# Single PSUM banks for the first two feed-forward units, and a new written order, in a BigBird attention and gated FFN kernel

## The chip, the core and the metric

The kernel runs on one core of a Trainium2 chip. The metric is the device time of one launch in microseconds (us). Before the change three runs took 278.1, 278.68 and 278.46 us, so the median is 278.46 us.

## The reference

Attention over 4 batches, 8 heads, 768 positions and 64 features per head, with a mask over blocks of 32 x 32 (a window of one block, the first and last block, and three sampled blocks per row of blocks), and behind it a feed-forward network (FFN) with a sigmoid gate on 3072 tokens of 512 features:

```python
scores = q @ k.T / 8;  scores = where(mask, scores, -1e9)
attn = exp(scores - max) / (sum + 1e-9);  x = (attn @ v) as tokens x 512
out = (sigmoid(x @ w_gate) * (x @ w_val)) @ w_out      # 512 -> 1536 -> 512
```

## The kernel before

**Units.** A unit is one batch and 256 queries; there are 12 of them, numbered 0 to 11 (three per batch). In a unit the 8 heads form 4 pairs, and each pair takes three key steps of 256 keys. A step is four score matmuls on TensorE (`scores`, through `tiled`, L352) into a PSUM tile of two banks, one exp of 128x1024 on ScalarE (L586), and one multiplication by the mask on VectorE (L592). Unit 0 does without that multiplication: its mask is a bias that four further matmuls add to the scores. A pair ends with its product with V (`pv` or `pv_parts`), a fold (L646) and a division (L656, the "norm").

**FFN.** When the four pairs of a unit are transposed into `xT`, jobs `f` compute gate and value columns: 16 matmuls with 512 columns out per bank, then a tanh (ScalarE, L801) and the gate (VectorE, L804), both on 128x512. Jobs `y` multiply by `w_out`; an evacuation (L886 or L888) and a store follow. Units 0 to 3 have FFN groups of their own, the others go in groups of two. Unit 0's FFN and the V products of units 0 and 1 use the whole 128x128 array, everything else of weight uses row tiles of 64 rows, two at a time.

**Masks and inputs.** The mask tiles are built by matmuls and copied to SBUF (`mask_tiles`, through the helper `copy`: L297 on ScalarE, L299 on VectorE). For batch 0, GpSimd's DMA queue brings q, k, v and the weights in the order of `FIRST`; TensorE transposes q and k (L467, L472), and VectorE copies V into `vex` (`vcopy`, L545). For batches 1 to 3 the loads are spread over the batch before them; VectorE lays two heads side by side (`pair_up`, L525, the "pair copy" into `qp` or `kp`) and SyncE's queue transposes that into `qT` or `kT` by DMA (`xbar`, L536). The same queue transposes `x` into `xT` from unit 2 on (L706) and stores the output (L878).

**PSUM.** Four tiles m0 to m3 of two banks each. Every job takes one of them and holds it until its evacuation.

**Order.** Nothing here is scheduled by the program at build time: some 1170 tasks are issued in the order of the string `ORDER`. A token is a task number, perhaps with an engine's letter, a PSUM tile after a colon, and after an @ the task that a load has to wait for. Tokens that begin with j are idle matmuls at the start. Each engine therefore takes its own instructions in the order in which `ORDER` names their tasks, and waits by semaphores for the others. The costs beside the tasks, such as `(PE, F_HALF)`, are left over from the search that wrote the string; they set nothing in the program that is built.

```python
self.last[i] = fn(eng or engines[0][0])
if gate is not None:
    self.hold(self.last[i], self.last[int(gate)])
```

Of the kernel before, what the change touches and what calls it, by code (L numbers as in the profile page):

```python
# [22 lines left out]
NT = S // 128  # L23
# [8 lines left out]
PE, ACT, DVE, DMA, SP = "PADGS"  # L32
# [4 lines left out]
EARLY = 2  # L37
# [3 lines left out]
j3 j3 j3 j3 j3 j3 j3 j3 5A 8D j3 0 11A j3s 9:0 j3s j3s j3s 10D j3s j3s 12:1 1:2 j3s 13A 3:0 2 j3s 34:1 4D 35 15:2  # L41
j3s 32:3 16D 6:0 33 17:1 7D 117:2 18D 97:0 118D 44:1 98A j3s 22:3 78:2 23D 45 36:0 79D 20:3 37 21D
40:2 25:1 30:3 41 26D 76:0 77D 46:1 31 54:2 19 74:0 47 75D 27:3 24 55 50:0 28D 80:1 64:3 51 81D
48:2 65 60:1 49 56:0 61 14 66:3 58:2 67D 105@30 57 29 89:3 59 38:1 90 52:0 86:2 53D 87 39 68:3
93:0 69D 62:1 108:2 94 42:3 109 43D 102:0 63D 111:3 70:1 103 110 126:2 71D 112 104 95:0 84:1 96D
122:3 85A 113 140:0 127 123 91 130:1 128 132:3 141 129 131 72:2 119:0 99:1 73D 133 120 147:2 134
100 135 142 157:0 148 154:3 171:1 124 155 149 158 88 164:3 143:2 156 176:0 92@164 144 121 146@111
101 172 170@44 165 173 161:2 217@54 145 190:1 177 189@46 162 125@40 178 237@54 159 186:3 191 150:2
115:0 151D 192 174:2 187 116 204:1 175 188 231:0 179:3 183:2 232 205 180D 244:3 184 233 206 166
245 82:0 200:2 218 83D 201 246 234:3 193:0 219 194A 152 235 185 153 211:2 136:0 220 137D 212 138  # L50
272:3 195 139 229 223A 202 167:0 255:2 168 236 273 213 221A 239 214:0 230 307:1 274 169 215 275
256 240 216 197:3 308 257 196 181 198 258 248:0 309 182 199 241:2 249 242 310 268:3 262 225:1 250
260 114@268 263 269 251 252:2 226 318:0 261 207:3 319 253 315:1 208 289:2 316 160@315 254 106:0
265:3 243 290 107A 247@265 266 270 276:1 209 291 300:0 293:3 277 301 278 282:1 294 292 283 297 163
303:0 335:2 295 302 222 304 279 227 285:1 336 296 286 238 359:0 305 337 360 210 284 331:3 228
362:1 348 332 361 264 349 363 333 328:0 287 350 329 267 322:3 351A 320 344:1 353A 311:0 323
203@344 345 341:2 387:3 321@359 312 342 317 271@282 426:1 373:0 313 411@300 427 330 397:2 374 398
343 388 346 375 259 408:1 376 389 355:2 400@268 409 390 347@30 419:0 356 334@89 380:3 405:1 428
370:2 381 306@111 364 420 288@44 406 371 386@214 366:3 421 410 365@265 454:2 422 433:1 455 432@380
# [3 lines left out]
442 474:1 484:0 463A 378 465A 339 467:2 452 340 475 524:3 480 485 525 514 354 515:1 327 468 486  # L63
# [4 lines left out]
538 583 438 550:1 567 571 542 439 586 551 638:0 563:2 572 425 539 564 552 595:1 573A 404 577:2 604  # L68
639 574 596 578 609:0 568 597 555 575A 627:2 598 616:3 610 628 617 543@616 635:1 565 712@200 630:2
611 569@300 636 612 592:3 446@563 688:0 631 593 658@60 689 654 706:1 556@231 588:3 707 579 641@550  # L70
640 642:0 632 676@471 619:1 633 589 587@282 620 594 691@214 623:2 690 613 590 670:1 591 643 671
637 605:3 624 644 621 606 645 659:1 618 625 709:0 681:3 710 626 660 607 655:2 682 692:0 656 453
663:3 711 726@99 661 657 608@234 673:2 693 662 674 622@652 664 672 694 548 699:1 695 665 723:2 666
# [3 lines left out]
762 669 782 730:3 745A 734:0 760 757:2 731 735 753 798:3 703 758 799 732 736 764:0 759 750 743A  # L77
600 765 797 826:3 823:1 767 763 824 650 816:0 766 651 827 809:1 756 768 810 719 800 787:3 817 769
733 788 806:1 801:0 807 770D 819:3 789 772A 811 737:1 790:2 839 738 614 802 580 615 791 803 601
# [5 lines left out]
904 856 925 936:0 978:1 913 937 911 857 919:3 979 908 875:0 920 914 876 929:1 921 917A 905 932  # L85
970:3 930 935 971 877 922 946:0 915A 1024:3 931 947 893 1025 928 1027:2 1012:0 939 938 916 1013
948 959:3 1028 966 1040:0 940 960 1041 1026 941 967:2 973:3 944A 942D 968 945 1029 952:0 1001:1
# [6 lines left out]
1078 1074 1094 1008 1082 1095 1083 1084 1100:1 1087A 1096A 1108:3 1088 1098A 1101 1085A 1099 1097  # L94
# [19 lines left out]

class Bank:


    def __init__(self):
        self.slot = None


class Plan:

# [13 lines left out]
    def run(self):  # L137
        done = set()
        for token in self.order:
            if token[0] == "j":  # L140
                self.idle(int(token[1]), token[2:])
                continue
# [1015 lines left out]
```

## Time and profile before

| | before |
|---|---|
| median of three runs | 278.46 us |
| span of the profiled execution | 277.8 us |
| TensorE (PE) busy | 270.0 us, 97%, 5007 matmuls |
| VectorE (DVE) busy | 207.1 us, 75%, 421 instructions |
| ScalarE (ACT) busy | 192.1 us, 69%, 243 instructions |
| GpSimd (POOL) busy | 47.3 us, 17% |
| granted TensorE clock | 1.00 from the start up to 240 us, 0.99 behind |

The profiled execution has a span of 277.8 us; the median lies 0.66 us above it, for what lies around the span and for the difference between executions. Matmuls overlap, so the duration of one is not what it adds: the pace is read from the distance of two starts. In the timeline a row "x6" stands for six instructions in a run, and the brackets at its end name the idle time ahead of it and what ended it.

### The profile page before, as it was taken

How to read it: one execution, taken by the hardware profiler on the slowest of the kernel's cores; microseconds unless marked ns; L12 is line 12 of the kernel's file. 1: busy time of each engine (PE TensorE's matmuls, PEld its weight loads, DVE VectorE, ACT ScalarE, POOL GpSimd, SP SyncE). 2: the span in 40 equal slices, each digit the busy share in tenths (PEclk: the TensorE clock that was granted, in tenths of full speed). 3: DMA queues.
4: the chain of work that ended last, by engine and by line, in shares of the span. 5: the costliest groups of instructions: out<-in, count | busy, mean ns of one | idle time of the engine just before them, and what ended most of it. 6: DMA issues, size and time to landing. Idle time of an engine off the chain costs nothing.

```text
span 277.8 us, 11169 instructions
## 1 busy us (share of the span) xinstructions
PE 270.0 (97%) x5007; PEld 178.7 (64%) x5007; DVE 207.1 (75%) x421; ACT 192.1 (69%) x243; POOL 47.3 (17%) x69
## 2 busy tenths in 40 slices
PE   8879999999999999999999999999999999999995
PEld 3667785896897798655566655655655676555543
DVE  4667788899999989978988886887876899004422
ACT  3988868899989958968868965679688571035300
POOL 7776261030480000028300000000000000000000
PEclk9999999999999999999999999999999999999999
DMA  7999999994599693339986743014130002230004
GB/s 160 175 195 197 200 205 198 140 139 100 84 160 145 117 140 97 103 98 167 142 113 113 73 61 97 2 21 142 24 96 4 4 2 76 70 151 2 0 2 151
DMA packets 56684, 28.93 MB, mean 104 GB/s; under 512 B 33036, under 2 KB 53692, under 8 KB 56636
## 3 DMA queue, kind: packets, MB, share of 16 engines
q0 software_dynamic: 21520, 13.90, 35.7%
q1 hardware_dynamic: 34628, 14.02, 24.8%
q8 instruction: 39, 0.64, 1.0%
q10 hardware_dynamic: 488, 0.30, 0.3%
q14 instruction: 9, 0.07, 0.1%
HBM read 28.47 MB, written 6.29 MB: 125 GB/s over the span
## 4 chain that ended last, share of the span: by engine, by line
PE 87%; DMA 7%; POOL 2%; ACT 1%; DVE 1%; issue 1%; SPq 0%
PE m L352 86%; DMA q<-in_q_dram 3%; DMA v<-in_v_dram 2%; DMA kT<-kp 1%; ACT P L586 1%; POOL k L226 1%; POOL q L226 1%; POOL wg L236 0%; POOL wv L236 0%; DVE ysb L888 0%; DVE P L592 0%; ACT ysb L886 0%; PE m L472 0%; PE m L467 0%; ACT ysb L929 0%
## 5 line engine op out<-in xcount | busy, mean ns | idle before, releaser
L586 ACT ACTIVATE P<-m 128x1024 f16<-128x1024 f32 x144 | 143.1, 1025 | 27.8 <-PE m L352 24.6
L352 PE MATMUL m<-xT,wg 64*128 64x512 f16 (+2 forms) x720 | 136.7, 326 | 0.1
L352 PE MATMUL m<-xT,wv 64*128 64x512 f16 (+2 forms) x720 | 136.7, 326 | 0.0
L592 DVE TENSOR_TENSOR P<-P,mask 128x1024 f16<-128x1024 f16 x132 | 87.0, 684 | 2.7 <-ACT P L586 2.6
L352 PEld LDWEIGHTS <-wg 64*128 64x128 f16 (+1 forms) x720 | 66.6, 94 | 21.2 <-issue 0.8
L352 PEld LDWEIGHTS <-wv 64*128 64x128 f16 (+1 forms) x720 | 66.4, 94 | 18.2 <-issue 0.5
L804 DVE SCALAR_TENSOR_TENSOR ht<-th,m 128x512 f16<-128x512 f32 x72 | 49.0, 685 | 37.0 <-ACT th L801 36.1
L352 PE MATMUL m<-wo,ht 64*128 64x512 f16 (+2 forms) x564 | 70.4, 372 | 0.0
L801 ACT ACTIVATE th<-m 128x512 f32<-128x512 f32 x72 | 42.8, 598 | 29.6 <-PE m L352 26.1
L352 PE MATMUL m<-qT,kT 64*128 64x256 f16 x576 | 53.6, 269 | 0.9 <-DMA kT<-kp 0.5
L352 PEld LDWEIGHTS <-P 64*128 64x128 f16 (+1 forms) x2112 | 41.1, 94 | 5.2 <-issue 0.4
L352 PEld LDWEIGHTS <-ht 64*128 64x128 f16 (+1 forms) x564 | 29.4, 94 | 23.4 <-issue 1.3
L352 PE MATMUL m<-vex,P 64*128 64x65 f16 (+1 forms) x2112 | 42.5, 190 | 0.0
L352 PEld LDWEIGHTS <-kT 64*128 64x128 f16 x576 | 26.7, 94 | 17.8 <-issue 1.3
L646 DVE TENSOR_REDUCE acc<-m 128x260 f32<-128x520 f32 x40 | 27.8, 697 | 7.9 <-PE m L352 6.8
L226 POOL DMA_DIRECT2D k<-in_k_dram x15 | 11.1, 744 | 48.3 <-PE m L352 45.0
L886 ACT ACTIVATE ysb<-m 128x512 f32<-128x512 f32 x18 | 10.2, 601 | 11.8 <-PE m L352 11.8
L656 DVE TENSOR_TENSOR x<-acc,rz 128x256 f16<-128x256 f32 x40 | 17.0, 425 | 1.4
L226 POOL DMA_DIRECT2D v<-in_v_dram x16 | 11.6, 736 | 33.5 <-PE m L352 12.9
L226 POOL DMA_DIRECT2D q<-in_q_dram x19 | 13.9, 733 | 3.9 <-DMA wo<-in_moe_w_out_dram 1.8
L352 PE MATMUL m<-bias,e 64*128 64x256 f16 x48 | 5.9, 271 | 2.3 <-DVE mask L299 1.9
L929 ACT ACTIVATE ysb<-m 128x256 f32<-128x256 f32 x1 | 0.4, 383 | 10.1 <-PE m L352 10.1
(47 smaller groups left out, 84.1 us busy)
## 6 DMA issues: line engine op xcount, KB each, us to landing
out_dram<-ysb SPq DMA_DIRECT2D x23, 256.0 KB, 2.4
v<-in_v_dram POOLq DMA_DIRECT2D x16, 192.0 KB, 5.1
k<-in_k_dram POOLq DMA_DIRECT2D x15, 192.0 KB, 6.6
q<-in_q_dram POOLq DMA_DIRECT2D x12, 192.0 KB, 6.4
wg<-in_moe_w_gate_dram POOLq DMA_DIRECT2D x6, 256.0 KB, 8.4
wv<-in_moe_w_val_dram POOLq DMA_DIRECT2D x6, 256.0 KB, 9.0
wo<-in_moe_w_out_dram POOLq DMA_DIRECT2D x3, 512.0 KB, 12.8
xT<-x SPq DMA_TRANSPOSE x40, 2.4
```

The costliest lines, as they stand in the source:

```text
L226: return nc.gpsimd.dma_start(dst[:, h0:h1, t0:t1, :], src[b, h0:h1].rearrange("h (p t) d -> p h t d", t=NT)[:, :, t0:t1, :],)
L352: return nc.tensor.matmul(out, lhsT, rhs, start=start, stop=stop, skip_group_check=True).ins
L586: nc.scalar.activation(self.pt.rearrange("a h i n -> a (h i n)"), both(self.bank).rearrange("a h n -> a (h n)"), AF.Exp, bias=0.0, scale=SCALE
L592: nc.vector.tensor_tensor(self.pt, self.pt, m.unsqueeze(1).broadcast_to([128, 2, 2, UQ]), op=ALU.mult,)
L646: nc.vector.tensor_reduce(self.acc.rearrange("a h s d -> a (h s d)"), self.parts.rearrange("a r n -> a n r"), axis=mybir.AxisListType.X, o ...
L656: nc.vector.tensor_tensor(self.x16.rearrange("a s h d -> a h s d"), self.acc[:, :, :, 0:D], rz.broadcast_to([128, 2, 2, D]), op=ALU.mult,)
L801: nc.scalar.activation(th, both(bank)[:, 0, :], AF.Tanh, bias=0.0, scale=0.5)
L804: nc.vector.scalar_tensor_tensor(self.ht[:, tiles[0] : tiles[-1] + 1, :], in0=th.rearrange("a (f n) -> a f n", n=self.w), scalar=1.0, in1= ...
L886: nc.scalar.activation(ysb, both(bank)[:, s, :], AF.Copy, bias=0.0, scale=0.5)
L929: nc.scalar.activation(ysb, src, AF.Copy, bias=0.0, scale=0.5)
```

## The change

- **PSUM** becomes one tile `m` of eight banks. A slot 0 to 3 is a pair of banks as before; a slot a to h is one bank.
- **FFN of units 0 and 1** (`SMALL` = 2) goes by a new job `f1`: one block of 128 gate and value columns in one bank, 8 matmuls of the whole array with 256 columns each, a tanh of 128x256 and a gate of 128x256. There are 24 such jobs for 12 jobs before. Unit 1 changes from row tiles to the whole array by it. The first four jobs of unit 0 (`EARLY`) are split, six matmuls on the first three pairs and two on the fourth.
- **Single banks** are also taken by the V products of units 0 and 1, by the transposes of TensorE (one 128x128 transpose instead of four 64x64 ones, where the string says so), by some mask tiles and by the last outputs.
- **The pair copy** of a batch now depends on the DMA transpose of the same heads of the batch before (`turned_b`).
- **The costs** of the search are replaced by other numbers, and `ORDER` by another string: idle tokens go from 19 to 12, one large evacuation (`mb24`) goes from VectorE to ScalarE, and GpSimd's loads get other tasks to wait for.

The core of the diff, without the string and the numbers:

```diff
-EARLY = 2
+EARLY, SMALL = 4, 2
...
-    units_ps = [ps.tile([128, 2, 512], f32, name=f"m{i}") for i in range(4)]
+    banks = ps.tile([128, 8, 512], f32, name="m")
+    units_ps = [banks[:, 2 * i : 2 * i + 2, :] for i in range(4)]
...
+    def one(bank):
+        i = "abcdefgh".index(bank.slot)
+        return units_ps[i // 2][:, i % 2, :]
...
+    rings["th1"] = [t[:, c : c + UQ] for t in rings["th"] for c in (0, UQ)]
...
+            if bank.single:
+                if flat:
+                    nc.tensor.transpose(one16(bank)[:, i * 128 : (i + 1) * 128], tile_, ident)
+                    continue
...
+        def f1(self, f):
+            bank = Bank()
+            i = len(used["th1"])
+            th = home("th1", i)
+            def go(cs):
+                def mm(eng):
+                    for c in cs:
+                        for g in range(2):
+                            bank.last = tiled(
+                                one(bank)[:, g * UQ : (g + 1) * UQ],
+                                (wg, wv)[g][:, c, f * 128 : (f + 1) * 128],
+                                self.x[:, c, :],
+                                c == 0 and g == 0,
+                                c == 3 and g == 1,
+                            )
+                return mm
+            def tanh(eng):
+                nc.scalar.activation(th, one(bank)[:, 0:UQ], AF.Tanh, bias=0.0, scale=0.5)
+            def gate(eng):
+                nc.vector.scalar_tensor_tensor(
+                    self.ht[:, f, :], in0=th, scalar=1.0,
+                    in1=one(bank)[:, UQ : 2 * UQ], op0=ALU.add, op1=ALU.mult,
+                )
...
         def f(self, j):
+            if self.g < SMALL:
+                for f in range(self.per * j, self.per * (j + 1)):
+                    self.f1(f)
+                return
...
-            a = pair_up(nm, *((k16, kp) if nm == "k" else (q16, qp)), b, p, [ld] + old)
+            a = pair_up(nm, *((k16, kp) if nm == "k" else (q16, qp)), b, p, [ld] + old + turned_b.get((nm, p), []))
...
+            turned_b[nm, p] = [c]
```

**VectorE, the first V copies (about 11 to 18 us of the profile before).** `vex0<-v16` is a copy of one pair's V behind its load, `mask<-m` a mask tile's evacuation, `x16n` the norm of pair n of unit 0. Before:

```order
L299 CAST mask_75<-m0_129 128x2x256
L545 COPY vex0_84<-v16_83 128x12x64
L299 CAST mask_75<-m0_129 128x2x256
L545 COPY vex0_84<-v16_83 128x12x64
L299 COPY qT0_86<-m3_132 128x2x2x64
L299 CAST mask_75<-m1_130 128x2x256
L655 RECIPROCAL rz_477<-m2_131 128x4
L656 TENSOR_TENSOR x161_149<-m2_131,rz_477 128x2x2x64
```

And after the change, at the same place:

```order
L304 CAST mask_75<-m_129 128x2x256 x2
L581 COPY vex0_84<-v16_83 128x12x64
L304 CAST mask_75<-m_129 128x2x256 x2
L581 COPY vex0_84<-v16_83 128x12x64
L691 RECIPROCAL rz_435<-m_129 128x4
L692 TENSOR_TENSOR x160_145<-m_129,rz_435 128x2x2x64
```

Before, the first copy is that of pair 1 (task 19), whose V is loaded second, and pair 1 is the first to be divided. After, it is that of pair 0 (task 14), and pair 0 (`x160`) goes first. All four first mask casts stand ahead of or just behind the first copy on VectorE, and none stands among the first exps on ScalarE any more, which now has the cast of `mb24` ahead of its first exp.

**SyncE's queue, the last transposes of batch 2 (about 105 to 120 us before).** `qT0` and `kT0` are the transposed q and k of batch 2, `xT` the transposed x of the FFN, `out` a store. Before:

```order
L706 DMA_TRANSPOSE xT1_160<-x165_153 128x2x128
L706 DMA_TRANSPOSE xT1_160<-x163_151 128x2x128
L706 DMA_TRANSPOSE xT1_160<-x164_152 128x2x128
L536 DMA_TRANSPOSE qT0_86<-qp_81 128x6x128
L536 DMA_TRANSPOSE kT0_88<-kp_82 128x6x128
L878 DMA out_0_dram<-ysb2_164 128x512
```

After:

```order
L572 DMA_TRANSPOSE kT0_88<-kp_82 128x6x128
L741 DMA_TRANSPOSE xT0_156<-x162_147 128x2x128
L572 DMA_TRANSPOSE kT0_88<-kp_82 128x6x128
L572 DMA_TRANSPOSE qT0_86<-qp_81 128x6x128 x2
L966 DMA out_0_dram<-ysb2_161 128x512
L741 DMA_TRANSPOSE xT1_157<-x164_149 128x2x128
L741 DMA_TRANSPOSE xT1_157<-x160_145 128x2x128
```

Before, the last q and k of batch 2 stand behind ten rows of `xT1` transposes and stores that follow the other six; after, all eight of batch 2 stand ahead of the `xT1` transposes.

**VectorE, the first gates (about 27 to 35 us before).** `ht0<-th` is a gate, `P<-P,mask` a multiplication by the mask. Before:

```order
L592 TENSOR_TENSOR P2_135<-P2_135,mask_75 128x1024
L592 TENSOR_TENSOR P13_146<-P13_146,mask_75 128x1024
L804 SCALAR_TENSOR_TENSOR ht0_157<-th0_154,m2_131 128x2x256
L655 RECIPROCAL rz_741<-m1_130 128x4
L656 TENSOR_TENSOR x165_153<-m1_130,rz_741 128x2x2x64
L299 COPY qT0_86<-m2_131 128x2x4x64
L804 SCALAR_TENSOR_TENSOR ht0_157<-th1_155,m3_132 128x2x256
```

After:

```order
L628 TENSOR_TENSOR P12_142<-P12_142,mask_75 128x1024
L834 SCALAR_TENSOR_TENSOR ht0_154<-th1_152,m_129 128x256
L834 SCALAR_TENSOR_TENSOR ht0_154<-th0_151,m_129 128x256
L691 RECIPROCAL rz_672<-m_129 128x4
L692 TENSOR_TENSOR x164_149<-m_129,rz_672 128x2x2x64
L628 TENSOR_TENSOR P2_132<-P2_132,mask_75 128x1024
L834 SCALAR_TENSOR_TENSOR ht0_154<-th1_152,m_129 128x256
```

Each gate has become two of half the width. Counted down VectorE's whole list in units of a full gate (two small ones are one), the 18th gate has 45 mask multiplications ahead of it in both kernels, the 24th has 60 before and 64 after, the 30th 75 and 78, the 42nd 99 in both: in between the new order runs attention ahead of the FFN. TensorE's matmuls are 5007 before and 4837 after, the difference being transposes and idle matmuls; its changes between row tiles, whole array and the small transposes' tiles are 39 before and 41 after.

More of the change, by code (lines that the diff above doesn't have):

```diff
@@ L31 @@
 NU = S // UQ
-PE, ACT, DVE, DMA, SP = "PADGS"
+PE, ACT, DVE, DMA, SP, ONE = "PADGSQ"
 VB = 5
@@ L429 @@
         ),
-        [(DVE, 0.42)],
+        [(DVE, 0.335)],
     )
     t_rows = [
-        rows(S, lambda eng, spread: copy(eng, mb24, spread), [(DVE, 0.95), (ACT, 0.82)])
+        rows(S, lambda eng, spread: copy(eng, mb24, spread), [(DVE, 0.87), (ACT, 0.70)])
     ]
@@ L438, in mask_tiles, with half @@
         bank = Bank()
+        w = c1 - c0
+        def half(i):
+            return one(bank)[:, i * w : (i + 1) * w] if bank.single else both(bank)[:, i, 0:w]
         def mm(eng):
@@ L744, in scores @@
         a = plan.add(
-            [(PE, (0.44 if first else 0.22) * len(run))],
+            [(PE, (0.433 if first else 0.217) * len(run))],
             mm,
@@ L753, in scores @@
             e = plan.add(
-                [(ACT, 0.98)], st.exp, [a] + before("P", 3 * pr.i + st.j), free=st.bank
+                [(ACT, 0.903)], st.exp, [a] + before("P", 3 * pr.i + st.j), free=st.bank
             )
@@ L844, in f @@
                     take=bank,
-                    lag=GAP,
-                    ops=16 * self.per,
+                    needs=wneeds,
                 )
                 a = plan.add(
-                    [(PE, F_HALF)], half(False), [a], ops=16 * self.per
+                    [(PE, 0.863 if self.w == 512 else 0.872)], half(False), [a], turn=True
                 )
             used["xT"][self.g].append(a)
-            c = plan.add([(ACT, 0.57)], tanh, [a] + before("th", i), free=bank, part=1)
-            g = plan.add([(DVE, 0.68)], gate, [c], free=bank, part=1)
+            old = before("th", i)
+            if i < len(rings["th"]) and used["th1"]:
+                old = [x for m in (2 * i, 2 * i + 1) for x in used["th1"][max(k for k in used["th1"] if k % 6 == m)]]
+            c = plan.add([(ACT, 0.477)], tanh, [a] + old, free=bank)
+            g = plan.add([(DVE, 0.598)], gate, [c], free=bank)
             used["th"][i] = [g]
@@ L898, in part @@
                     take=bank if first and f0 == 0 else None,
-                    lag=0.0 if f0 < 8 else GAP if first else None,
-                    ops=16,
+                    turn=not first and f0 == 0,
+                    needs=(f"o{f0 // 4}",),
                 )
@@ L940, in store @@
                 [after],
[L941 removed]
+                dma="O",
             )
@@ L970, in y_last @@
                         take=bank if f0 == 0 else None,
-                        lag=0.0 if f0 < 8 else None,
-                        ops=8,
-                        wide=True,
+                        one=True,
+                        mode="W",
                     )
```

308 lines of the change are left out of this document (170 added, 138 removed), and 49 rows, old and new, of the table ORDER.

## The prediction

> **What bounds the kernel now.** I read the page first, then TensorE's waits, then the start of the timeline, then a table of stretches. The page:
>
> ```profile
> span 277.8 us, 11169 instructions
> PE 270.0 (97%) x5007; PEld 178.7 (64%) x5007; DVE 207.1 (75%) x421; ACT 192.1 (69%) x243; POOL 47.3 (17%) x69
> PE   8879999999999999999999999999999999999995
> ```
>
> TensorE is busy for 97% of the span and, from the fourth of the forty slices (21 us) to the last but one, for nine tenths or more of each. So the time is TensorE's own work plus what it waits; the change can win at the start, in a few waits, and nowhere else, because it leaves TensorE's arithmetic as it is. The waits of TensorE (total, times, longest):
>
> ```profile
> PE m L352 <- DVE mask L299: 1.9, 1, 1.9
> PE m L329 <- DVE junk L206: 1.0, 1, 1.0
> PE m L352 <- DMA kT<-kp: 0.5, 1, 0.5
> PE m L352 <- DVE x L656: 0.3, 1, 0.3
> PE m L472 <- DMA q<-in_q_dram: 0.2, 1, 0.2
> ```
>
> One wait of 1.9 us for a mask cast is half of all. The timeline shows how it comes about, beginning with a piece of the chain of waits (the landing of the first pair's V), and what it does to ScalarE:
>
> ```profile
> 6.34 6.93 DMA v<-in_v_dram
> ...
> 6.73 1.94 ACT L586 ACTIVATE P<-m 128x1024 f16<-128x1024 f32 x2 [0.86 <-PE m L352]
> 8.56 0.59 ACT L297 CAST mask<-m 128x512 f16<-128x512 f32 x1
> 9.17 5.69 ACT L586 ACTIVATE P<-m 128x1024 f16<-128x1024 f32 x6
> 14.35 0.36 DVE L545 COPY vex<-v 128x768 f16<-128x768 f16 x1 [1.53 <-DMA v<-in_v_dram]
> 14.63 0.68 DVE L299 CAST mask<-m 128x512 f16<-128x512 f32 x1
> 15.36 0.29 PE L352 MATMUL m<-bias,e 64*128 64x256 f16 x2 [1.91 <-DVE mask L299]
> 16.01 4.82 ACT L586 ACTIVATE P<-m 128x1024 f16<-128x1024 f32 x5 [1.15 <-PE m L352]
> 23.94 0.28 PE L352 MATMUL m<-xT,wg 128*128 128x256 f16 x1
> ```
>
> V of the first pair has landed at 6.34 + 6.93 = 13.27 us, yet VectorE stands until 14.35 for the V of the second, which it copies first; a mask cast is queued behind the copy, TensorE waits for the cast's PSUM tile until 15.36, and ScalarE then waits 1.15 us for scores. The twelve exps of unit 0 are pushed back by that and by the cast at 8.56, and the first FFN matmul starts at 23.94.
>
> **The start.** After the change VectorE copies V of pair 0 first, the casts of ScalarE among the exps are gone, and TensorE takes the V product of pair 0 first. Within a run the exps follow each other by (5.69 - 1.03) / 5 = 0.93 us (one takes 1.03, the group row below). If nothing interrupts them the twelfth ends at 6.73 + 11 x 0.93 + 1.03 = 18.0 us. Before, it is the fourth of the run at 16.01, with (4.82 - 1.03) / 4 = 0.95 us each: 16.01 + 3 x 0.95 + 1.03 = 19.9. The gap of 1.9 is the most that the start can give, and agrees with TensorE's wait of 1.91. Two things are taken off. ScalarE now casts `mb24` (128x768) ahead of its first exp; its 128x512 cast took 0.59, and it was idle 0.86 us ahead of that exp, so I charge 0.15 for the part that may not fit. And TensorE will still wait a little, for the third pair's transposes or for the casts that now stand ahead of the first copy: V lands at 13.27, a copy of 0.36 and a cast of 0.68 can still come one behind the other ahead of TensorE's next job, so that I charge 0.45, between nothing (the V product is queued late enough) and 1.04 (copy and cast both late). That makes -1.9 + 0.15 + 0.45 = **-1.3 us**, from -1.9 to -0.7. The weights hold it up no further: TensorE waits for none of them in the list above, and the first FFN job only comes from 23.9 to about 22.
>
> **The small jobs.** TensorE's work is the same: 8 matmuls of 256 columns on the whole array, for half of 16 on half of the rows with twice the columns. What the split costs lies on the evacuating engines:
>
> ```profile
> L801 ACT ACTIVATE th<-m 128x512 f32<-128x512 f32 x72 | 42.8, 598 | 29.6 <-PE m L352 26.1
> L929 ACT ACTIVATE ysb<-m 128x256 f32<-128x256 f32 x1 | 0.4, 383 | 10.1 <-PE m L352 10.1
> L804 DVE SCALAR_TENSOR_TENSOR ht<-th,m 128x512 f16<-128x512 f32 x72 | 49.0, 685 | 37.0 <-ACT th L801 36.1
> 5.60 0.42 DVE L427 TENSOR_SCALAR bias<-m 128x256 f16<-128x256 f32 x1 [0.21 <-PE m L413]
> 30.00:65.00 35.00, 35.00 (x691) 28.01 (x691) 30.19 (x63) 29.81 (x39) 7.85 (x11) 1.00 1.17 170
> ```
>
> The trace has no gate of 128x256; its nearest rows are the 0.42 of a VectorE operation on 128x256 from PSUM and ScalarE's 0.383. Twenty-four small ones for twelve: VectorE 24 x 0.42 - 12 x 0.685 = +1.9 us, ScalarE 24 x 0.383 - 12 x 0.598 = +2.0 us. These jobs lie in the stretch from 30 to 65 us (columns of the last row: time, length, then busy of PE, PEld, DVE, ACT, POOL, the clock, DMA), where VectorE is idle for 35 - 30.19 = 4.8 us and ScalarE for 5.2. So I cost them at nothing; half a PSUM tile also comes free sooner. If the cover is gone, all of it, 2 us, is late.
>
> [...]
>
> **The V products, transposes and changes of mode.** The V products of units 0 and 1 keep their 24 matmuls. A change of the array's tiles costs TensorE something: in three rows on end,
>
> ```profile
> 25.05 0.27 PE L352 MATMUL m<-xT,wg 128*128 128x256 f16 x1
> 25.16 0.27 PE L352 MATMUL m<-xT,wv 128*128 128x256 f16 x1
> 25.36 0.23 PE L467 MATMUL m<-const,x 64*128 64x64 f16 x4
> ```
>
> starts are 0.11 us apart in one mode and 0.20 across the change: 0.09 us. There are 41 changes for 39, +0.2; from 0 (they fall where TensorE waits anyway) to 0.5, if the whole-array transposes, longer than the small ones, aren't hidden either. I take **+0.2 us**. [...]
>
> **The later waits.** Near 122 us TensorE waits for the last k of batch 2:
>
> ```profile
> 117.37 1.24 SPq L536 DMA_TRANSPOSE qT<-qp x1
> 118.66 1.29 SPq L536 DMA_TRANSPOSE kT<-kp x1
> 121.35 0.90 PE L352 MATMUL m<-vex,P 64*128 64x65 f16 x48
> 122.78 0.39 PE L352 MATMUL m<-qT,kT 64*128 64x256 f16 x4 [0.53 <-DMA kT<-kp]
> 200.00:240.00 40.00, 39.88 (x690) 24.50 (x686) 29.74 (x57) 22.43 (x29) 0.00 (x0) 1.00 0.15 44
> ```
>
> The transpose is issued at 118.66, done by 122.78. After, it stands ahead of the `xT1` transposes and stores that it followed, so I count the wait as gone: -0.53, and -0.1 for the run-out of the V product's pipeline in front of it. In the stretch from 200 to 240 us TensorE is short of 40 - 39.88 = 0.1 us, which may go too. Together **-0.7 us**, from -0.7 to 0 (another transpose late in its stead). The new dependency of the pair copy on the batch before holds up VectorE's queue only if that transpose is still under way; batches are some 60 us apart, so I cost it at nothing. What could be queued behind such a wait are mask multiplications.
>
> **VectorE between 87 and 111 us.** This is what speaks against the change:
>
> ```profile
> L592 DVE TENSOR_TENSOR P<-P,mask 128x1024 f16<-128x1024 f16 x132 | 87.0, 684 | 2.7 <-ACT P L586 2.6
> 33.52 2.49 DVE L592 TENSOR_TENSOR P<-P,mask 128x1024 f16<-128x1024 f16 x4
> 86.90 0.69 DVE L804 SCALAR_TENSOR_TENSOR ht<-th,m 128x512 f16<-128x512 f32 x1
> 111.16 0.69 DVE L804 SCALAR_TENSOR_TENSOR ht<-th,m 128x512 f16<-128x512 f32 x1
> 65.00:87.00 22.00, 22.00 (x498) 17.45 (x496) 20.59 (x40) 20.08 (x25) 8.62 (x12) 1.00 0.83 125
> 87.00:111.00 24.00, 24.00 (x642) 19.74 (x640) 22.36 (x48) 19.68 (x24) 0.00 (x0) 1.00 0.70 117
> ```
>
> The gates at 86.90 and 111.16 are the 18th and the 24th. Between them the new order puts four more mask multiplications on VectorE (60 to 64 ahead of the 24th, 45 ahead of the 18th in both). A run of four takes 2.49, so each adds (2.49 - 0.68) / 3 = 0.60 us: 4 x 0.60 = 2.4 us in a stretch in which VectorE is idle for 24 - 22.36 = 1.6 us. If all of that idle time can be used, 0.8 us are too much and gates come late by it, and TensorE with them; if none, 2.4. Work can also move into the stretch ahead, with 22 - 20.59 = 1.4 idle, which the small jobs' gates leave alone, and PSUM tiles in hand let TensorE run on. I take **+0.9 us**, near the lower end, because VectorE's idle time in this kernel mostly waits for something (the group rows: gates for the tanh 36.1 us) that comes earlier when TensorE is itself held.
>
> **Sum.** Of the profiled execution's 277.8 us: -1.3 + 0.2 - 0.7 + 0.9 = -0.9, so 276.9; the median of the runs shown is 0.66 above the span, 278.46, so 278.46 - 0.9 = 277.56, said as **277.6 us**. With the terms' good ends (-1.9, 0, -0.7, +0.8) it is 276.7, with the bad ends (-0.7, +0.5, 0, +2.4) 280.7. About 0.2%, 0.56 us, is what a measurement of this kernel can tell from no change.
>
> **Rivals.**
> 1. *VectorE becomes the bound between 65 and 115 us.* None of its idle time is usable, the four multiplications cost 2.4 us, and 0.9 of the 1.9 us of the small gates is pushed in front of them: 3.3 us for 0.9. Then the sum is -1.3 + 0.2 - 0.7 + 3.3 = +1.5: 280.0 us. For it: 93% busy in the stretch. Against it: the multiplications are ahead of need, so that a late one need not stop TensorE. It decides from about 2.4 us of waits, where the gains are used up. In the milder half of it, waits of some 2.6 to 2.9 us, 279.2. Chance 0.28.
> 2. *The start's gain is lost again.* TensorE meets another wait ahead of the first FFN matmul, for the second half of q (the waits list has 0.2 us for it even now) or for a bank that a small tanh still holds; the start gives 0.2 rather than 1.3, and the sum is +0.2: 278.6 us. For it: DMA is full in the first 40 us, and an earlier TensorE meets the same landings. Against it: 1.4 us of waits for weights or q would have to appear where 0.2 are. Chance 0.14.
> 3. *One tile instead of four.* If waits were made for the whole tile `m` rather than for its banks, each job would wait for every other's evacuation, and the banks would not be independent: the change would not do what it says, and the time would rise by tens of us, since each exp of 1.03 us would stop TensorE. The order's waits show none of this kind, so only 0.02, outside the range.
>
> The forecast's own case, with 276.7 to 278.4 as its range, has the remaining 0.56; in a part of it, 0.07, the waits at VectorE are 1.5 to 1.9 and the time is within 0.2% of before. The bounds: **276.6 to 280.0 us** reach to the first rival. Faster by over 0.2%: 0.49. Within: 0.07, with 0.10 of the second rival: 0.17. Slower by over 0.2%: 0.28 + 0.02 + 0.04 = 0.34.
>
> **What the profile after would show.** Right: no idle TensorE of over 0.6 us between 12 and 16 us; twelve exps on end from 6.7 to 6.9 us on ScalarE; the first FFN matmul at 22 to 22.7; no wait for `kT<-kp` at 120; waits for VectorE of about 0.9 us between 87 and 120. Wrong: the first FFN matmul at 23.5 or later (second rival); waits for mask multiplications or gates of over 2.4 us in the list (first rival); a `qT` or `kT` wait at another place, which would bring back the 0.7.

## The result, and the profile after

| | before | after |
|---|---|---|
| median of four runs | 278.57 us | 289.34 us |
| runs | 278.1, 278.46, 278.68, 278.98 | 285.49, 286.62, 292.06, 293.16 |
| ratio, 95% interval | | 1.026 (1.0218 to 1.0303) |
| span of the profiled execution | 277.8 us | 284.9 us |

The forecast was 277.6, with 280.0 as its upper end: it is wrong, in sign and in range. Two runs of after (292.06, 293.16) had a granted clock of 0.99 on average and are left out of the ratio, which would be 1.039 with them (289.34 / 278.57); the profiled one, 286.62, is not one of them.

The page of after, with the fortieths of the span for TensorE (PE) and for the DMA engines:

```profile
span 284.9 us, 10851 instructions
PE 272.2 (96%) x4837; PEld 182.9 (64%) x4837; DVE 208.8 (73%) x433; ACT 192.2 (67%) x255; POOL 47.2 (17%) x69
PE   8999999979887998999999999999999999999995
DMA  8999999999999999540310133002221001330003
```

No engine has become the bound by its work: VectorE's busy time went from 207.1 to 208.8, ScalarE's stayed. But TensorE's row has holes between the ninth and the thirteenth slice (57 to 93 us) and in the sixteenth (107 to 114 us), and up to the sixteenth the DMA row is full. A table of stretches of after (time, length, busy of PE, PEld, DVE, ACT, POOL, clock, DMA) shows how much:

```profile
0.00:30.00 30.00, 28.14 (x483) 20.84 (x485) 21.01 (x56) 26.21 (x34) 22.15 (x34) 1.00 1.27 183
30.00:60.00 30.00, 28.63 (x518) 22.44 (x513) 25.63 (x61) 23.03 (x38) 10.07 (x15) 1.00 1.32 184
60.00:90.00 30.00, 25.79 (x515) 19.76 (x516) 24.81 (x56) 24.27 (x30) 6.38 (x9) 1.00 1.33 170
90.00:120.00 30.00, 27.96 (x693) 25.08 (x690) 27.41 (x56) 23.18 (x30) 7.87 (x11) 1.00 1.21 154
120.00:150.00 30.00, 30.00 (x604) 19.68 (x602) 25.39 (x49) 23.43 (x31) 0.72 (x1) 1.00 0.24 50
```

The same for before:

```profile
30.00:60.00 30.00, 30.00 (x573) 23.95 (x573) 25.33 (x52) 24.91 (x33) 7.14 (x10) 1.00 1.20 175
60.00:90.00 30.00, 30.00 (x690) 23.51 (x688) 28.42 (x60) 27.58 (x34) 9.33 (x13) 1.00 0.88 127
90.00:120.00 30.00, 30.00 (x746) 23.39 (x744) 27.13 (x58) 25.37 (x31) 0.00 (x0) 1.00 0.56 113
```

From 30 to 120 us TensorE now idles 1.37 + 4.21 + 2.04 = 7.6 us, where it idled none. And GpSimd's column tells what else is new: before, it issues no load between 90 and 120 us; after, 11. The waits of TensorE in after (total, times, longest):

```profile
PE m L366 <- issue: 3.1, 4, 1.4
PE m L366 <- DVE ht L905: 1.7, 2, 1.5
PE m L366 <- DVE ht L834: 1.7, 1, 1.7
PE m L366 <- DVE P L628: 1.0, 2, 0.7
```

There are two kinds: 4.4 us for gates and mask multiplications of VectorE, and 3.1 us of "issue", a wait for nothing that the profile shows. VectorE was itself held, by its waits for loads:

```profile
DVE qp L561 <- DMA q<-in_q_dram: 2.9, 1, 2.9
DVE kp L561 <- DMA k<-in_k_dram: 2.8, 2, 2.2
DVE vex L581 <- DMA v<-in_v_dram: 0.7, 1, 0.7
```

The timeline shows one of these as a chain, from GpSimd's load through VectorE's pair copy to TensorE:

```profile
51.73 1.43 POOL L231 DMA_DIRECT2D k<-in_k_dram  x2
58.80 0.62 DVE L561 COPY kp<-k 128x768 f16<-128x768 f16 x1 [2.15 <-DMA k<-in_k_dram]
59.87 0.41 DVE L834 SCALAR_TENSOR_TENSOR ht<-th,m 128x256 f16<-128x256 f32 x1
60.34 0.27 PE L366 MATMUL m<-xT,wg 128*128 128x256 f16 x1 [1.71 <-DVE ht L834]
```

The first of these two loads, a k of batch 1 issued at 51.73, lands 7 us later. VectorE stands 2.15 us before the copy; the gate of unit 1 that is queued behind it starts at 59.87, though its tanh had ended at 56.43, and TensorE waits 1.71 us for the gate's bank. At 85.19 the same happens with a q of batch 2 that was issued at 75.55.

### The profile page after: what moved, and what is told of

It reads as the page before. It is cut to its first block, busy times and chain, and to the rows that moved or that the text cites. A ratio compares the mean times of both kernels' runs of the same rounds, so it can differ in the third digit from the quotient of the medians.

```text
span 284.9 us, 10851 instructions
## 1 busy us (share of the span) xinstructions
PE 272.2 (96%) x4837; PEld 182.9 (64%) x4837; DVE 208.8 (73%) x433; ACT 192.2 (67%) x255; POOL 47.2 (17%) x69
## 4 chain that ended last, share of the span: by engine, by line
PE 83%; DMA 8%; issue 3%; POOL 2%; DVE 2%; ACT 0%; POOLq 0%; DVEq 0%
PE m L366 82%; DMA q<-in_q_dram 5%; DMA v<-in_v_dram 3%; POOL k L231 1%; DVE P L628 1%; POOL q L231 1%; POOL v L231 0%; DVE ht L905 0%; PE m L489 0%; DVE acc L682 0%; PE m L499 0%; PE m L502 0%; DVE x L692 0%; ACT ysb L1016 0%; DVE e L212 0%
## 5 line engine op out<-in xcount | busy, mean ns | idle before, releaser
L366 PEld LDWEIGHTS <-wg 64*128 64x128 f16 (+1 forms) x672 | 62.3, 94 | 22.4 <-issue 2.5
L366 PEld LDWEIGHTS <-wv 64*128 64x128 f16 (+1 forms) x672 | 62.4, 94 | 21.7 <-issue 3.5
L905 DVE SCALAR_TENSOR_TENSOR ht<-th,m 128x512 f16<-128x512 f32 x60 | 40.9, 686 | 37.8 <-ACT th L902 37.4
L902 ACT ACTIVATE th<-m 128x512 f32<-128x512 f32 x60 | 35.6, 597 | 32.3 <-PE m L366 28.2
L366 PEld LDWEIGHTS <-ht 64*128 64x128 f16 (+1 forms) x564 | 31.3, 94 | 23.5 <-issue 2.1
L366 PEld LDWEIGHTS <-kT 64*128 64x128 f16 x576 | 28.5, 94 | 16.1 <-issue 4.2
L831 ACT ACTIVATE th<-m 128x256 f32<-128x256 f32 x24 | 9.0, 399 | 6.8 <-PE m L366 4.9
L834 DVE SCALAR_TENSOR_TENSOR ht<-th,m 128x256 f16<-128x256 f32 x24 | 9.1, 416 | 1.3 <-ACT th L831 1.3
```

The source lines that it names most:

```text
L366: return nc.tensor.matmul(out, lhsT, rhs, start=start, stop=stop, skip_group_check=True).ins
L831: nc.scalar.activation(th, one(bank)[:, 0:UQ], AF.Tanh, bias=0.0, scale=0.5)
L834: nc.vector.scalar_tensor_tensor(self.ht[:, f, :], in0=th, scalar=1.0, in1=one(bank)[:, UQ : 2 * UQ], op0=ALU.add, op1=ALU.mult,)
L902: nc.scalar.activation(th, both(bank)[:, 0, :], AF.Tanh, bias=0.0, scale=0.5)
L905: nc.vector.scalar_tensor_tensor(self.ht[:, tiles[0] : tiles[-1] + 1, :], in0=th.rearrange("a (f n) -> a f n", n=self.w), scalar=1.0, in1= ...
```

## The experiments

Two theories: **loads** (L), that GpSimd's loads of batches 1 to 3 now lie under SyncE's transposes and each stretches the other; **instructions** (F), that the pauses "issue" are TensorE without instructions, whose fetch is behind the loads. Against them stand the prediction's own rival (VectorE has too much to do) and the changes of banks and order by themselves.

For several kernels I give a **lag**: by how much a matmul of TensorE starts later than all of TensorE's work ahead of it would take back to back, at the pace of each kind of matmul in undisturbed stretches. Lag grows only where TensorE loses time. The paces are fitted, and another fit makes the rises up to 0.8 us smaller, so differences of less than that say little.

| lag (us) at | 30 | 60 | 90 | 120 | end |
|---|---|---|---|---|---|
| before | 8.2 | 8.3 | 8.4 | 8.5 | 9.7 |
| after | 6.3 | 6.4 | 13.3 | 16.2 | 16.4 |
| after, loads small (e1) | 8.3 | 8.4 | 9.9 | 10.2 | 10.4 |
| after, loads moved (e10) | 7.1 | 7.2 | 7.7 | 8.9 | 9.4 |

**Are the loads the cause?** The loads of both later batches (2 and 3) an eighth as large, everything else of after untouched:

```diff
+        rows = slice(0, 128 if b < 2 else 16)
-            dst[:, h0:h1, t0:t1, :],
+            dst[rows, h0:h1, t0:t1, :],
```

> The changed kernel, but the loads of q, k and v of batches 2 and 3 bring only 16 of the 128 partitions (so an eighth of their bytes; the attention of these batches is computed from stale data). Nothing else is changed. Theory L (the loads of batch 2 lie under the DMA transposes of batch 1; both land late, and VectorE stands before its pair copies): transposes between 50 and 90 us land in 3 to 4.5 us instead of 9, VectorE's waits for loads of batch 2 go, TensorE's idle time from 60 to 118 us falls from some 7.5 to under 2 us, and the span is 276 to 278 us. Rival V (VectorE has too much to do, 12 more gates and the multiplications drawn ahead): the span stays above 282 us with waits for gates and multiplications. Rival G (it is GpSimd's gates, the loads are issued too late whatever their size): VectorE's waits for loads stay at more than half of their 6.4 us.

Measured: 278.46, ratio 0.9991 (0.9964 to 1.0019). The whole loss is gone, and VectorE's waits for loads fall from 6.4 to 1.5 us; so by themselves neither VectorE's work, nor the banks, nor the small jobs, nor the order of TensorE cause it. The DMA view from 50 to 90 us, (count, median us from issue to landing), before:

```profile
q0 software_dynamic: 4083, 2.95, 55.2%
q1 hardware_dynamic: 8053, 2.17, 33.7%
xT<-x SPq DMA_TRANSPOSE x8, 3.1
```

after:

```profile
q0 software_dynamic: 4139, 3.00, 71.5%
q1 hardware_dynamic: 12026, 3.60, 60.9%
kT<-kp SPq DMA_TRANSPOSE x7, 6.0
xT<-x SPq DMA_TRANSPOSE x7, 9.2
```

and with small loads:

```profile
q0 software_dynamic: 1718, 1.11, 25.1%
kT<-kp SPq DMA_TRANSPOSE x8, 3.9
xT<-x SPq DMA_TRANSPOSE x7, 5.4
```

The loads (q0) bring the same 3.0 MB in these 40 us before and after. What is new is the transposes (q1) in the same stretch, 12,026 packets for 8,053: packets of both queues take longer (a packet of q0 0.111 us for 0.087, of q1 0.032 for 0.027, from the shares of 16 engines and the counts), and the transposes of x 9.2 us for 3.1. The transposes alone do not do it: with small loads q1 brings even more packets in this stretch, 13,439, and the lag rises 1.5 us from 60 to 90 instead of 6.9. But its transposes of x still take 5.4 us, above the 3 to 4.5 expected, so not all of the 9.2 is the loads.

Then batch 2's loads alone small (`rows` 16 for `b == 2`), and batch 3's alone:

> The changed kernel with only the loads of batch 2 small (16 of 128 partitions; the attention of batch 2 is computed from stale data); those of batch 3 are whole. Theory L: the waits between 60 and 90 us go, the pauses between 97 and 120 us, under the loads of batch 3, stay: 280 to 282 us. If one batch's traffic alone does not matter, either all of the loss stays or all of it goes (278.5).

> The changed kernel with only the loads of batch 3 small (16 of 128 partitions; the attention of batch 3 is computed from stale data). Complement of the run with batch 2's loads small. Theories L and F: the waits at 60 and 72 us stay, those behind 87 us lessen, the pauses at 100 and 112 us go: 282 to 285 us. If the loads of batch 3 do not matter, 286 us.

With batch 2's small: 280.6, 1.0049 (1.0014 to 1.0084), as expected; the lag rises 1.3 us from 60 to 90 instead of 6.9, and a pause of 1.1 us near 106 stays. With batch 3's small: 286.62, 1.0249 (1.0206 to 1.0293), a miss; by the time alone the other branch, 286, came out. The trace speaks against that branch: behind 100 us it is as flat as expected (lag 16.7 to 16.9 up to 120). But from 60 to 90 us this execution loses 8.5 us, and its granted clock is 0.5 from 89.4 to 92.8 us (its gate matmuls on row tiles start 0.21 us apart there, 0.11 at full clock), right behind 3.4 us in which TensorE was busy for only 1.47; after has no such stretch of low clock. So the two don't add up to the whole. Why the loss at 60 to 90 is larger here than in after, whose loads up to 80 us are of the same size, isn't shown.

**Is the place of the loads enough?** The banks and the order of before, with only six loads of batch 3 issued at 94 us, under transposes, instead of from 123:

```diff
+ 543@474 556 587 658 641 608
- 543@616 ... 658@60 ... 556@231 ... 641@550 ... 587@282 ... 608@234
```

> The kernel before, with six loads of batch 3 (k and q of three pairs) issued at about 94 us, among the DMA transposes of batch 2, instead of at 123 us and later. Theory L: the transposes between 91 and 105 us take 5 us or more to land instead of 2.5 to 3.3, the scores of batch 2 wait for them, and the time rises by 0.5 to 2 us. Rivals V and G: the loads are off every path, and the time stays within 0.3 us of before.

Measured: 289.75, 1.0402 (1.0332 to 1.0472): moving six loads in the old kernel costs more than the change itself, and far more than the 0.5 to 2 us expected. The DMA view from 94 to 110 us of before and of this kernel, then its waits and its stretches:

```profile
kT<-kp SPq DMA_TRANSPOSE x3, 3.3
```

```profile
kT<-kp SPq DMA_TRANSPOSE x3, 9.1
```

```profile
PE m L351 <- DMA kT<-kp: 4.0, 2, 2.8
PE m L351 <- issue: 3.2, 1, 3.2
```

```profile
100.00:105.00 5.00, 2.93 (x89) 2.44 (x83) 4.90 (x10) 2.43 (x4) 0.00 (x0) 1.00 1.59 151
105.00:110.00 5.00, 1.24 (x9) 0.59 (x9) 0.43 (x1) 1.02 (x1) 0.00 (x0) 0.54 1.34 150
110.00:115.00 5.00, 4.75 (x70) 3.68 (x72) 1.29 (x2) 1.62 (x2) 0.00 (x0) 0.50 1.07 147
115.00:120.00 5.00, 5.00 (x136) 4.36 (x132) 3.31 (x8) 3.63 (x5) 0.00 (x0) 0.94 0.23 76
```

A transpose of k takes 9.1 us where it took 3.3 before; TensorE stands, and then has half its clock from 105 to 115 us: in the row from 110 to 115 it is 95% busy with 70 matmuls. The lag rises 10.9 us from 100 to 140 us: 7.2 are the waits of the list, and the other 3.7 are left for the slow clock. The same move with the six loads small, with two of the loads only, and with two only while the others are kept back behind task 616:

```diff
+ 543@474 556
- 543@616 ... 556@231
- 712@200
+ 712@616
```

The last two lines are those that only the third of them has.

> The kernel before with the same six loads of batch 3 issued at 94 us as in the kernel that lost 4%, but all loads of batch 3 bring only 16 of 128 partitions (the attention of batch 3 is computed from stale data). Theory L (the loss is their traffic under the transposes): 278 to 279.5 us, no pause of TensorE of over 1 us between 100 and 112 us. If the loss came from the moved tokens (queue order, a semaphore), it stays at 288 us.

> The kernel before with only two loads of batch 3 (k and q of one pair) at 94 us instead of six. Theory L with a price for each load: a third of the 4% of six, 3 to 4 us. If a margin decides (the transposes of batch 2 land 2 to 5 us before their scores need them), the time stays within 0.5% of before.

> The kernel before with two loads of batch 3 at 94 us, and the other ten held back to 123 us as in the kernel before (the edit before took that gate away with the first token, so that they came at 116 us under the last transposes). Theory L, from the part of the trace of that run up to 112 us: +1.5 us, 279.5 to 280.7 us. If its whole 2.3% came from the two, 284 us or more.

Small: 281.38, 1.0113 (1.0066 to 1.016), against 1.0402, so most of the loss is the loads' traffic; the transposes of k take 3.3 us again, and the pause and both long waits are gone. The time itself missed its range, 278 to 279.5: the profiled execution, 278.53, is the fastest, and what the others lose (281.2 to 283.3) isn't shown. Two: 285.82, 1.023 (1.0173 to 1.0287), above both branches. I had overlooked that the gate of the two also kept the others back: those came at 116 us, under the last transposes of batch 2, and 3.7 of its 4.0 us of waits for k are there. Two, others kept back: 279.37, 1.0031 (1.0007 to 1.0055). So two loads in this place cost 0.9 us, of which the trace shows one pause of 1.0 us, and six cost 11: by these two points the price of a load grows with their number; of the 11, 3.7 are what is left for the slow clock (the mean clock of this execution is 0.982, and 0.999 with two loads, where the one pause is of 1.0 us).

**Can the change be had without the loss?** In after I moved the loads and what hangs on them, first in two simple ways. The first issued the loads of batches 1 to 3 in groups and moved the copies and transposes of batch 2 back behind them; the second put nine pair copies just 2.5 us ahead of their transposes and left the loads, but for four that have to follow these copies. Parts of the two edits:

```diff
- 366@200 ... 181@200 353@200 ... 443@292 295@292 314@292
+ 181@264 ... 114@200 171@200 ... 295@343 314@343 353@343 366@343
```

```diff
- 371 ... 358 ... 456 306 ... 328 ... 410 ... 424 ... 470
+ 306 ... 456 ... 328 ... 371 ... 358 ... 410 ... 424 ... 470
```

> The changed kernel with the loads of batches 1 to 3 regrouped on GpSimd's queue: the last loads of batch 1 ahead of those of batch 2, batch 2 from about 66 to 83 us, batch 3 from about 110 us, and the pair copies and transposes of batch 2 (and four of batch 3) moved back on VectorE and SyncE so that each stands some 10 us behind its load. Everything else, small jobs and attention order, as in the changed kernel. Theory L: 276.5 to 279 us, with the start as in the changed kernel (first FFN matmul at about 21 us). Rival V: over 281 us.

> The changed kernel with nine pair copies (eight of batch 2, one of batch 1) moved back in the order, each to about 2.5 us ahead of its transpose, and with four loads that have to follow them; loads, transposes and all else stay where they are. If the loss is VectorE standing in order before copies whose loads have not landed (theory L, first half), its waits for loads of 6.4 us fall under 1.5 us, TensorE's waits for gates and multiplications between 60 and 90 us (5.4 us in the changed kernel) fall under 1 us, and the time is 280 to 282 us; the pauses of TensorE that nothing explains (3.1 us) stay. If late transposes or the pauses are the loss, the time stays over 284 us.

Both missed, badly: 292.5, 1.0489 (1.0415 to 1.0563), and 294.73, 1.0571 (1.0519 to 1.0624). The first wait of each list, of the first kernel and of the second:

```profile
PE m L365 <- DMA xT<-x: 4.7, 3, 2.1
```

```profile
PE m L365 <- DMA xT<-x: 9.0, 3, 5.1
```

Neither after nor before has this wait. SyncE issues its transposes in the order of the list too: in the first kernel three norms of x end at 74.9, 76.1 and 84.1 us, but SyncE issues their transposes from 97.5 us on, behind five transposes of q and k whose copies VectorE ends only between 87.6 and 92.4. So a transpose of q or k that waits for its copy, or for a late load behind that, held the transposes of x behind it, for which TensorE then waits 4.7 us. The remedy must keep both queues free of waits. So, in two steps: batch 1's last loads ahead of batch 2's, batch 2's in two groups at 63 and 74 us, batch 3's behind the last transposes, and each copy 8 us or more behind its load; then all of it again some microseconds finer (V of batch 1 at 55 us, batch 3 from 124):

```diff
- 366@200 ... 181@200 353@200 ... 171@292 114@292 ... 443@292 295@292 314@292
+ 181@264 ... 114@302 171@302 ... 223@292 ... 295@330 314@330 353@330 366@330
+ 397@415 418@415 443@415 464@415 ... 336@595 379@595 432@595 478@595
+ 575@659 588@659 ... 673@720 690@720 723@720 744@720
```

> The changed kernel with the loads of batch 2 in two groups of four (about 63 and 74 us) and its V at 103 us, batch 3 from 118 us on, the last loads of batch 1 ahead of them all, and the copies and transposes of batch 2 moved so that each follows its load by some 8 us and none stands ahead of a transpose of x that is needed earlier. Theory L: 276.5 to 280 us, and at or below the kernel before if the transposes land in under 5 us. If the small jobs and the attention ahead of need are the loss, over 282 us.

> As the second regrouping of the loads, with three shifts: V of batch 1 at 55 us instead of 50 (behind most of batch 1's transposes), the first four loads of batch 2 at 65 instead of 63, and batch 3 from 124 us instead of 118 (behind the transposes of x that the FFN needs at 119). Theory L: the waits of the second regrouping at 57, 93 to 100 and 120 to 140 us (2.4 us together) halve, and the time is 278 to 280 us; under 278 it would beat the kernel before. If the loads are no longer what is left, it stays at 281.5.

281.55, 1.0105 (1.0073 to 1.0137), a miss between the two branches, and 279.41, 1.0022 (0.9996 to 1.0048), within its range: the second takes back the loss, with no pause left, and is the same as before within its interval. It isn't faster.

A last step (the q of pair 3 transposed later, some copies moved) went wrong in an instructive way, and its repeat with batch 2's V loads small tests the theory of the instructions:

```diff
- 27Q:e 22Q:f 23 28 ... 410 ... 424 ... 456 ... 470
+ 22Q:f 23 ... 27Q:e ... 28 ... 410 ... 424 ... 456 ... 470
```

> The third regrouping with two more shifts: the last pair's q of batch 0 is transposed four PE jobs later (TensorE waited 0.6 us for its landing at 10.9 us), and the pair copies of pairs 2 and 3 of batch 2 are taken out of the place on VectorE ahead of 85 and 93 us, where TensorE waits for folds (0.3 and 0.4 us). If these waits are what is left, 278.0 to 278.8 us; if ScalarE's exps set the start's pace, the first shift gives nothing and it stays at 279 to 279.4.

> The fourth regrouping (280.75 us, all of its loss one pause of TensorE of 2.1 us at 115 us that no semaphore explains) with the four loads of V of batch 2, which run from 107 to 114 us there, bringing only 16 of 128 partitions (batch 2's output is computed from stale V). Theory F (TensorE has run out of instructions: the packet that fetches the next 16 KB of them stands behind the loads): the pause goes, 278.3 to 279 us. If the pause comes from something else at that place, it stays, 280 to 281.

280.75, 1.0088 (1.0061 to 1.0114), a miss by one pause of 2.1 us near 115 us (and the 0.6 us that the first shift was to take came back as a wait for a mask cast); with small V loads 279.26, 1.0006 (0.9982 to 1.0031), and no pause. The DMA view from 107.7 to 115 us of the first:

```profile
q0 software_dynamic: 1050, 0.76, 111.7%
q1 hardware_dynamic: 830, 0.41, 25.3%
```

of the kernel without that step (e10), and of the one with small loads:

```profile
q0 software_dynamic: 1011, 0.73, 72.8%
q8 instruction: 1, 0.02, 0.8%
```

```profile
q0 software_dynamic: 57, 0.03, 4.0%
q8 instruction: 1, 0.02, 1.1%
```

Only the kernel that pauses has no packet of q8, the queue of instructions, in these 7 us; its next one starts at 115.06, and the pause lasts from 115.37 to 117.52. Counted in its trace, TensorE had run 493 instructions (weight loads and matmuls) since the packet before, 500 at the pause of the six early loads; otherwise a packet mostly comes every 200 to 300.

The places of the pauses say it more sharply. The kept traces have 14 pauses "issue" of over 0.15 us, in nine kernels. Each begins when TensorE has run 705, 2753, 3521, 4033, 4289 or 4545 instructions, and these six numbers lie whole multiples of 256 apart. Each ends 1.2 to 1.6 us after a packet of 16 KB has landed. Counted off in order, a packet starts at most 296 instructions ahead of the place where its block begins, 221 in the median, and 0 to 102 at the pauses. And q8 brings 39 packets of 16 KB in before, for 10,014 weight loads and matmuls, and 38 in after, for 9,674: one for 257 and one for 255. So I read a pause as TensorE at the end of a block of 256 instructions, with the next one fetched late. What holds the packet up ahead of its start, no record shows: that it stands behind the loads is inferred from the pauses that go with small loads.

**Two terms by themselves**, each in the kernel before. The first V copies behind the mask casts (the start), and the last pair's copies and transposes earlier (the wait at 122 us):

```diff
- 54:2 19 74:0 ... 27:3 24 55
+ 81D 19 48:2 65 60:1 24 49
```

```diff
- 547 424 ... 583 438 ... 542 439 ... 572 425
+ 379 424 425 438 439
```

> The kernel before with one part of the change alone: VectorE's copies of V of pairs 1 and 2 behind the mask casts that were queued behind them (two tokens of the order moved). By the prediction's reading of the start, the 1.9 us wait of TensorE at 13.4 us goes, some 0.5 us of it comes back behind it, and the time falls by 1.0 to 1.6 us, to about 277.2 us. If ScalarE's exps set the pace there, it falls by less than 0.5 us.

> The kernel before with one part of the change alone: the pair copies and DMA transposes of the last pair of batch 2 (k and q) are moved from behind ten transposes of x and stores to right behind the other pairs' (four tokens). By the prediction, the wait for k at 122 us goes: -0.5 to -0.7 us, 277.6 to 277.9 us against 278.3. If two more transposes ahead of the transposes of x make those late (theory L), no gain or a loss.

The first: 279.77, 1.0031 (1.0009 to 1.0053), where a gain of over 1 us was expected; the branch of less than 0.5 came out. In its profiled execution, its fastest (278.38), the wait for the mask is 0.6, and a wait of 0.9 for the V copy has come in its stead. Why its other runs mostly take a microsecond or more longer stays open. The second: 280.57, 1.0055 (1.0028 to 1.0083), no gain either, as its other branch had it. The wait at 122 is gone, but TensorE waits 2.5 us near 112 us for an evacuation, and VectorE says why:

```profile
111.99 0.43 DVE L656 TENSOR_TENSOR x<-acc,rz 128x256 f16<-128x256 f32 x1 [2.96 <-DMA xT<-x]
```

The norm overwrites an `x` that a transpose has still to read, and that transpose now stands behind the ones pulled forward.

## Why the prediction was wrong, point by point

**The step that failed is a term that is missing.** The sum has no term for GpSimd's loads of the later batches. The text ahead of it says that they get other tasks to wait for, and the prediction asked of the transposes and copies only whether they come earlier: the gain at 122 us, and the pair copy's new dependency, "I cost it at nothing" (which held: what VectorE waits for ahead of its pair copies is loads). It never set the new issue times of the loads beside the transposes and the copies that hang on them. That was to be had: before, batch 2's loads lie between 72 and 83 us, and no load is issued under the transposes behind them, from 83 to 123.

```profile
81.88 0.76 POOL L226 DMA_DIRECT2D q<-in_q_dram  x1
123.48 0.72 POOL L226 DMA_DIRECT2D k<-in_k_dram  x1 [40.84 <-PE m L352]
```

After, they lie between 51 and 107 us, and those of batch 3 from 75 us on. The term was worth about 8 us: from 30 to 120 us the lag of after rises 9.9, that of e10 1.8.

**The start** was over-sized, on one execution. The first FFN matmul of after starts at 20.95 for 23.94, and its lag at 30 us is 1.9 less than before's, more than the forecast -1.3; of the second rival only a wait of 0.5 us for q shows, at 10.28. But the mask wait of 1.9 on which the term rests is not typical. Two of the kernels that begin with the same instructions as before (the six small loads, the two gated ones) have in their wait lists the lines below, and the other three have 0.6 to 0.9:

```profile
PE m L352 <- DVE mask L299: 0.6, 1, 0.6
```

```profile
PE m L351 <- DVE mask L298: 1.0, 1, 1.0
```

Over six profiles with the start of before the lag at 30 us is 7.0 to 8.2, in the mean 7.5; over eight with the start of after 6.2 to 8.3, in the mean 6.7. So about -0.8 (-0.5 by the other fit), not -1.3, and the two ranges overlap. The profiled execution of before was longer than the median: the runs here have a time 1.7 to 1.9 us above their span (286.62 to 284.9), so that a span of 277.8 stands for some 279.6. The 0.66 that the prediction took for what lies around the span was the wrong offset; it drops out of the forecast, which is the median less 0.9.

**The small jobs** were right. The groups of after give 399 ns for the tanh (forecast 383) and 416 for the gate (420):

```profile
L831 ACT ACTIVATE th<-m 128x256 f32<-128x256 f32 x24 | 9.0, 399 | 6.8 <-PE m L366 4.9
L834 DVE SCALAR_TENSOR_TENSOR ht<-th,m 128x256 f16<-128x256 f32 x24 | 9.1, 416 | 1.3 <-ACT th L831 1.3
```

They cost nothing: in e1 and e10 TensorE loses 0.1 us between 30 and 60. Of the 170 matmuls fewer, which the text ahead of the prediction puts down to transposes and idle matmuls, 96 are unit 1's: its 192 on row tiles, starting some 55 ns apart, have become 96 on the whole array, 109 ns apart, which is the same time.

**The later waits** went as forecast in after (no wait for `kT<-kp`, no idle time behind 120 us). That the gain is free was wrong in general: by itself the edit brings a new wait of 2.5 us (e15); another transpose late in its stead was the bad end of this term, but at 0, not at a loss.

**VectorE between 87 and 111 us** was over-sized, as far as waits show it: with the loads cured TensorE waits for VectorE for 0.3 us (e10) and 0.2 us (e13) from 80 to 120, for a forecast of +0.9. The lag rises more there, 1.5 and 1.1 us against 0.15 before; what the rest of it is stays open. The first rival, VectorE as the bound, is refuted as the cause of the loss: after's waits for VectorE come behind VectorE's own waits for loads, and fall from 4.4 to 0.6 us with small loads.

**The sum without the loads** then is about -0.8 - 0.7 + 1.2 = -0.3 us, where the 1.2 is that rise of the lag and not VectorE's waits alone, and the changes of mode (+0.2 forecast), which no run measured apart, take most of that. So what was left to win is about what can't be told from no change: e1 and e13 show just that (0.9991, 1.0006), and e10 hardly more. With the 8 us of the loads it is some +7.8, for a measured +7.2 (1.026 of 278.57).

## What to carry to other kernels

When an order moves loads, lay their issue times beside the transposes and fetches of instructions that run in the same stretch, and beside the first instruction that waits for each and what is queued behind it: with the same 13.9 MB of loads on GpSimd's queue, after took 2.6% more than before and e10 0.2%. A moved group goes together (load, copy, transpose, first use), with as much room between them as a crowded load takes, here 7 to 8 us where it was 5 to 6 before. And a term read from one wait of one execution should be read from a second execution before it carries a sum.

## What the runs showed of the hardware that was not expected

- Transposes by DMA and plain loads took longer where they ran together. A transpose of k took 3.3 us, 9.1 with six loads of 192 KB under it, and 3.3 with the same six small. Those of x took 3.1 us before, 9.2 in after and 5.4 with small loads. The loads of q, k and v took 7.0 to 8.3 us in the median in after for 4.6 to 6.4 before, from 50 to 90 us.
- TensorE stopped 14 times, in nine kernels, for 0.2 to 3.2 us, with no semaphore to blame: each time after 705, 2753, 3521, 4033, 4289 or 4545 of its instructions, whole multiples of 256 apart. Each stop ended 1.2 to 1.6 us after a packet of q8 had landed. Those packets started 0 to 102 instructions ahead of the place, for 221 in the median of all. The pauses at two such places went when the loads around them were small (3.2 us in e3, none in e6; 2.1 in e11, none in e13).
- After waits of 3.2 and 2.8 us close together, the granted clock was half of full from 105.4 to 115.6 us (0.54 and 0.50 in the rows of 5 us from 105, 0.94 in the next). In the three thirds of these 10.2 us TensorE was busy for 1.24, 1.95 and 3.40 us of 3.4, and in the 3.4 us ahead of them for 0.93. With batch 3's loads small the clock was at half behind 3.4 us with 1.47 busy, from 89.4 to 92.8 us, while it stayed at full behind 1.69 of 3.4 in after (58.6 to 62.0 us) and 1.42 with the last pair earlier (111.7 to 115.1 us). So how much idle time brings the halving isn't shown, nor what ends it.
